# Two-layer attention and MLP in fp32 on one core: half of w_1's loads issued later, the last block's rows kept on chip for layer 2, the first two scores put in other banks

## The chip, the cores and the metric

The kernel runs on one core of one Trainium2 chip, in one launch. Its time is the device time of an execution in microseconds (us); the time before is the median of three runs. Five engines run their own instruction lists in order and meet at semaphores: PE (matrix products, weight loads listed apart as PEld), DVE (vector), ACT (scalar, activation), POOL (GpSimd) and SP, which here only issues DMA transfers.

## The reference

Two layers, each an attention block and an MLP with the same weights, on x of 2048 tokens by 640, all in fp32:

```python
x = x + _A_ref(_layernorm(x), A_wqkv, A_wo)                 # layer 1
x = x + _B_ref(_layernorm(x), B_w1, B_b1, B_w2, B_b2)
x = x + _A_ref(_layernorm(x), A_wqkv, A_wo)                 # layer 2
x = x + _B_ref(_layernorm(x), B_w1, B_b1, B_w2, B_b2)
# _A_ref: qkv = x @ wqkv, 32 heads of 20; o = softmax(q k^T / sqrt(20)) v; o @ wo
# _B_ref: h = x @ w1 + b1 (1536 wide); max(h, 0)^2 @ w2 + b2
```

## The kernel before

**Arithmetic.** Every factor of a product is kept as two parts, high and low, in a reduced fp32 form (`F32R`), and a product is the sum of three products of parts (`THREE`). So nearly all of the work is PE's.

**Stages of one layer.** (1) `qkv`: layer norm of four blocks of 512 tokens (`front`: load four 128-row tiles `x`, statistics at L244 and L245 on DVE and L247 and L248 on POOL, normalise at L252, 20 PE transposes at L398 into banks, and a split into `xnT`), then the projections to q, k and v (`product`, L327; v leaves its bank at L373). The projections of a tile stand in two row halves on PE, and a small ACT copy `mark_t` (L329) hands over between them. (2) Attention: a first pass of scores by queries (L479) only finds the row maxima (L491 on DVE straight from the bank, or L500 on ACT and L508 on DVE for pairs); the second pass computes scores by keys (`score`, L561), exponentials (L568, ACT) and the product with v (`pv`, L573), which accumulates in bank 7. (3) `add_heads`: the out-projection (L289) of four blocks of four row tiles, each row tile in two halves, each half added to the residual row by DVE from its bank (L1154). (4) `mlp`: four blocks of 512 tokens, each in two halves of the 1536: six groups of products with w_1 (L289 again, called by `mlp`), ReLU (L1224, ACT), square (L1225, DVE), split (L256, L257), then products with w_2 (L1239) and adds into the rows (L1250, DVE).

**From the out-projection to the MLP.** The rows of block 0 need layer norm and a turn by 90 degrees before the first w_1 product. `turn_out` does it in ten steps: per row statistics, normalise, a 32x32 transpose by DVE (L1186) into a tile `y`, and four scattered stores `d_t<-y`, issued one step after the transpose. `turn_in` then loads the five `xnT` tiles back (`xnT<-d_t`), in one step, and in five more steps casts each on ACT (L1202) and subtracts (L1203). These steps are a list, and `side()` runs the next one after each bank of the out-projection has been added. In the turn of block 0 this DVE work stands in between DVE's adds, in the order of the program.

**Order and resources.** There is no scheduler: instructions stand on each engine in program order, written out by hand. SP issues all loads and stores named here in its own order, at L76, and a transfer waits there for its data and for one of a small number of lanes. Weights w_1 (15 slots of 512 KB) and w_2 lie in 42 arena slots, with `xnT`, e, q, k and v; rows `x` and `y` share 11 slots of another pool. PSUM has eight banks. `Ring` hands out banks in turn: `ps_st` banks 0 to 3 for the scores by keys, `ps_pj` 4 to 7 for projections, `ps_q` 0 to 3 for maxima and transposes during `qkv`; in attention the maxima rotate over 4, 5, 6 (`sm_ring`). `ps_all` rotates over all eight in stages 3 and 4.

**Names of the change.** `loads` in `layer` lists which weights are loaded before which block of the out-projection; `loads[1]` is the second part of w_1. `ahead` is true in layer 1, where the MLP already prepares layer 2's projections: three of the four blocks are turned through memory during the last MLP block, and the fourth, block 3, is prepared by `second()`, called at the start of layer 2's `qkv`, with `front`, from the rows that the MLP stored to memory (`d_x`).

Of the kernel before, what the change touches and what calls it, by code (L numbers as in the profile page):

```python
# [39 lines left out]
def tile_layers(  # L40
# [29 lines left out]
    def dma(eng, dst, src):  # L70

        if dst.dtype == F32R:
            dst = dst.bitcast(F32)
        if src.dtype == F32R:
            src = src.bitcast(F32)
        eng.dma_start(dst, src)  # L76
# [291 lines left out]
    def end_v(tt, hf, dst):  # L368
        whole = tt in vs
        if not whole:  # L370
            vs[tt] = slot([P, H, 32], F32, "v")
            nc.gpsimd.memset(vs[tt][:, :, DH:], 1.0)
        nc.scalar.copy(  # L373
            vs[tt][:, hf * 16 : hf * 16 + 16, :DH],
            dst[:, :HALF].rearrange("p (h d) -> p h d", d=DH),
        )
        if whole:
            v = vs.pop(tt)
            return lambda: dma(nc.sync, d_v[tt * P : (tt + 1) * P], v)

    def front(tb, x_src, bank, each=1, on_pool=()):

        rows = [row_tile(x_src, tb * 4 + i) for i in range(4)]
        yield 0, False
        mvs = []
        for x in rows:
            mvs.append(stats(x))
            yield 1.1, False
        for n, (x, mv) in enumerate(zip(rows, mvs)):
            normalise(nc.vector, x, mv)  # L390
            yield 0.65, n == 3
        res = []
        for k0 in range(0, KD, each):
            ks = range(k0, min(k0 + each, KD))
            dsts = [bank("xt") for _ in ks]
            for k, dst in zip(ks, dsts):
                for i in range(4):
                    nc.tensor.transpose(  # L398
                        dst[:, i * P : (i + 1) * P], rows[i][:, k * P : (k + 1) * P], ident
                    )  # L400
            for k, dst in zip(ks, dsts):
                t = slot([P, 2, QB], F32R, "xnT")
                (split_on_pool if k in on_pool else split_to)(t[:, 0, :], t[:, 1, :], dst)
                res.append(t)
            if len(res) == KD:
                xt_[tb] = res
                rows.clear()
            yield 0, len(res) < KD
# [132 lines left out]
    def mrows_load(t):  # L541
# [7 lines left out]
            )  # L549
        done.add(t)  # L550

    def score(t, kt, h, es):

        p, par = divmod(h, 2)
        if p not in es:
            es[p] = weights[len(e_n) % len(weights)]
            e_n.append(t)
        dst = ps_st("st")
        b = 64 * par
        assert t in done  # L560
        nc.tensor.matmul(  # L561
            dst,
            k_t[t // NQB, kt // 4][b : b + 62, p, (kt % 4) * P : (kt % 4 + 1) * P],
            q_t[t][b : b + 62, p, :],
            start=True,
            stop=True,
        )
        nc.scalar.activation(es[p][:, par, :], dst, AF.Exp, scale=SCALE)  # L568
# [385 lines left out]
    def attention(first, x_src, first_rows):  # L954
# [135 lines left out]
        def pairs():  # L1090
# [8 lines left out]
            state["debt"] -= n  # L1099
            return n  # L1100

        for o in "abab":
            op(o)
        yield
# [101 lines left out]
    def new_rows():  # L1206
        return [slot([P, 2, QB], F32R, "xnT") for _ in range(KD)]

    def mlp(qb, xnt, x_mid, x_dst, side):

        xs = []
        for fh in range(2):
            hs = []
            for f in range(fh * 6, fh * 6 + 6):
                dst = ps_all("pu")
                chain(dst, [
                    (w_1.piece(f * 10 + hw * KD + k), xnt[k][:, hx, :])
                    for k in range(KD)
                    for hw, hx in THREE
                ])  # L1220
                if qb == NQB - 1:
                    w_1.past(f * 10 + 9)
                r = xtile("r")[:, :QB]
                nc.scalar.activation(r, dst, AF.Relu, bias=b1_t[:, f : f + 1])  # L1224
                nc.vector.tensor_mul(r, r, r)  # L1225
                h = slot([P, 2, QB], F32R, "h")
                split_to(h[:, 0, :], h[:, 1, :], r)
                hs.append(h)
                if fh == 0 and f in (1, 2, 3, 4):
                    x = row_tile(x_mid, qb * 4 + f - 1)  # L1230
                    nc.gpsimd.tensor_add(x, x, b2_t)
                    xs.append(x)
                side()
            f0 = fh * 6

            def part(dst, hf, i, fs):
                for f in fs:
                    for hx, hw in THREE:
                        nc.tensor.matmul(  # L1239
                            dst[:, :HALF],  # L1240
                            hs[f][:, hx, i * P : (i + 1) * P],
                            w_2.piece(at_2(f0 + f, hw, hf)),
                            start=(f == 0 and (hx, hw) == THREE[0]),
                            stop=(f == 5 and (hx, hw) == THREE[-1]),
                        )

            def add(dst, hf, i):
                c = slice(hf * HALF, (hf + 1) * HALF)
                x = xs[i]
                nc.vector.tensor_add(x[:, c], dst[:, :HALF], x[:, c])  # L1250
                r0 = (qb * 4 + i) * P
                if fh == 1 and qb * 4 + i == NKT - 1:
                    dma(nc.sync, x_dst[r0 : r0 + P, c], x[:, c])
                elif fh == 1 and hf == 1:
                    dma(nc.sync, x_dst[r0 : r0 + P, :], x)
                side()

            first_two = [ps_all("y") for _ in range(2)]
            for fs in (range(5), (5,)):
                for i in range(2):  # L1260
                    part(first_two[i], 0, i, fs)
            for i in range(2):
                add(first_two[i], 0, i)
            for hf in range(2):
                for i in range(0 if hf else 2, 4):
                    dst = ps_all("y")
                    part(dst, hf, i, range(6))
                    add(dst, hf, i)
            if fh == 0 and qb == NQB - 1:
                w_2.past(at_2(5, 1, 1))  # L1270

    def layer(first, x_a, x_m, x_e, front_0, ahead):
# [15 lines left out]
        def all_steps():  # L1288
# [3 lines left out]
        xnt, rows = [], []  # L1292
        loads = [
            [(w_1, s) for s in range(8)],
            [(w_1, s) for s in range(8, w_1.n)],
            [(w_2, s) for s in range(5)],
            [(w_2, s) for s in range(5, 10)],
        ]
        for qb in range(NQB):
            if qb + 2 == NQB:  # L1300
                xnt.extend(new_rows())
            add_heads(qb, x_a, x_m, xs, side, rows)
            if qb == 0:
                out_0 = turn_out(d_t[0], rows)
                steps.extend([lambda: next(out_0)] * 10)
                in_0 = turn_in(d_t[0], lambda: xnt)
                steps.extend([lambda: next(in_0)] + [None] * 2 + [lambda: next(in_0)] * 5)
            for sp, s in loads[qb]:
                sp.load(s)
            if qb + 1 == NQB:  # L1310
                all_steps()
# [3 lines left out]
        for qb in range(NQB):  # L1315
            new = []
            plan = [[] for _ in range(28)]

            def put(gen, *sides):
                for i in sides:  # L1320
                    plan[i].append(lambda: next(gen))

            def rows_of(src, tb):
                return lambda i: row_tile(src, tb * 4 + i)

            def to(where):

                def get():
                    where.extend(new_rows())
                    return where  # L1330

                return get

            d = d_t[(qb + 1) % 2]
            if qb + 1 < NQB:
                put(turn_out(d, rows_of(x_m, qb + 1)), *range(4, 14))
                put(turn_in(d, to(new)), 19, *range(22, 27))
            if ahead and qb:
                out_at = range(14, 24) if qb + 1 < NQB else range(2, 12)
                put(turn_out(d_t[1 + qb], rows_of(x_e, qb - 1)), *out_at)  # L1340
            if ahead and qb + 1 == NQB:
                for tb, at in enumerate((4, 14, 19)):
                    xt_[tb] = []
                    sub = nc.gpsimd.tensor_sub if tb == 2 else nc.vector.tensor_sub
                    put(turn_in(d_t[2 + tb], to(xt_[tb]), sub), at, *range(at + 3, at + 8))
                for n in range(5):
                    plan[20 + n].append(lambda n=n: w_qk.load(n))
            steps.extend((lambda p=p: [f() for f in p]) for p in plan)
            mlp(qb, xnt, x_m, x_e, side)
            xnt = new  # L1350
            if qb + 1 < NQB:
                all_steps()
# [4 lines left out]
    def second():  # L1357


        yield from front(3, d_x[1], ps_q, 2, (1, 3))  # L1360

    def constants():

# [97 lines left out]
```

## Time and profile before

| | us |
|---|---|
| median of the runs | 3607.83 |
| the runs | 3604.56, 3607.83, 3613.43 |
| the profiled execution | 3610.41 |
| its span | 3608.6 |
| PE busy in the span | 3583.8 (99%) |
| DVE busy | 2752.8 (76%) |
| ACT busy | 2650.0 (73%) |
| POOL busy | 803.7 (22%) |

A row of the timeline gives the start in us from the span's start, the busy time of the group, the engine, the line and operation, what it writes and reads, its shape and the count of instructions; in brackets stand the idle time of the engine ahead of it, in us, and what ended it. A row of the waits gives the waiting engine, what it wrote, its line, the releaser, and then the whole wait in us, the number of waits and the longest. Of this span 25 us lie outside of PE's busy time; the prediction looks for them by place.

### The profile page before, as it was taken

What the parts mean: (1) busy time and instruction counts of PE and PEld (TensorE: products, weight loads), DVE (VectorE), ACT (ScalarE), POOL (GpSimd) and SP (SyncE); (2) the same over time, 40 slices, a digit from 0 to 9 for tenths busy, and PEclk for the clock granted to TensorE, in tenths of its full rate; (3) what the DMA queues carried; (4) which work ended last, traced back from release to release, by engine and by line L of the source; (5) the groups of instructions that cost most, each with busy time, mean ns of one, the idle gap of its engine ahead of it and who ended that gap; (6) DMA issues with size and microseconds to landing.
All of it is one profiled execution on the core that took longest, in us unless ns stands there. A gap on an engine that the chain in (4) does not pass through costs nothing.

```text
span 3608.6 us, 67689 instructions
## 1 busy us (share of the span) xinstructions
PE 3583.8 (99%) x25562; PEld 2131.5 (59%) x25562; DVE 2752.8 (76%) x5081; ACT 2650.0 (73%) x5152; POOL 803.7 (22%) x880
## 2 busy tenths in 40 slices
PE   9999999999999999999999999999999999999999
PEld 7886434343434345999988963333443434368998
DVE  7877999999999993445567789999999999924443
ACT  3678999999999996122327789999999999942221
POOL 5531434311212211111144201211211211211110
PEclk9999999999999999999999999999999999999999
DMA  8866555323211125834577652222322111367221
GB/s 277 279 225 175 172 139 167 113 67 78 58 47 51 42 90 198 271 86 111 145 253 251 204 153 66 76 72 56 77 72 62 48 41 51 105 214 247 74 77 40
DMA packets 378117, 453.89 MB, mean 126 GB/s; under 512 B 176722, under 2 KB 224082, under 8 KB 377790
## 3 DMA queue, kind: packets, MB, share of 16 engines
q1 hardware_dynamic: 376974, 447.21, 41.4%
q8 instruction: 201, 3.29, 0.4%
q10 hardware_dynamic: 816, 2.36, 0.2%
q14 instruction: 126, 1.03, 0.1%
HBM read 275.14 MB, written 174.30 MB: 125 GB/s over the span
## 4 chain that ended last, share of the span: by engine, by line
PE 93%; DMA 3%; DVE 1%; POOL 1%; SPq 1%; ACT 1%; issue 0%; DVEq 0%; POOLq 0%; ACTq 0%
PE banks L573 27%; PE banks L561 19%; PE banks L479 16%; PE banks L289 12%; PE banks L327 9%; PE banks L1239 9%; SPq L76 1%; DMA q<-d_qk 1%; ACT e L568 0%; DVE bst L244 0%; PE banks L398 0%; DMA d_x<-x 0%; DMA few<-d_s 0%; DMA d_t<-y 0%; DMA o<-d_r 0%
## 5 line engine op out<-in xcount | busy, mean ns | idle before, releaser
L568 ACT ACTIVATE e<-banks 128x512 f32<-128x512 f32 x3968 | 2049.2, 604 | 67.7 <-PE banks L479 6.0
L491 DVE TENSOR_REDUCE mx<-banks 128x1 f32<-128x512 f32 x3076 | 1929.8, 683 | 211.7 <-PE banks L479 141.9
L479 PE MATMUL banks<-k,q 60*128 60x512 f32 x3586 | 1243.7, 428 | 2.9 <-DVE mx L491 1.4
L561 PE MATMUL banks<-q,k 62*128 62x512 f32 x3968 | 1116.6, 433 | 1.0 <-DVE mx L508 0.9
L573 PE MATMUL banks<-e,vg 128*32 128x512 f32 x8192 | 1091.0, 605 | 1.5 <-ACT e L1086 1.5
L561 PEld LDWEIGHTS banks<-q,k 62*128 62x128 f32 x3968 | 583.6, 185 | 656.0 <-ACT e L568 623.9
L479 PEld LDWEIGHTS banks<-k,q 60*128 60x128 f32 x3586 | 581.5, 184 | 292.0 <-DVE mx L491 217.6
L508 DVE CUSTOM_DVE_ANT_0 rl<-banks,rl 128x512 f32<-128x512 f32 x510 | 332.9, 688 | 102.2 <-PE banks L479 93.2
L327 PE MATMUL banks<-xnT,wqk 64*128 64x512 f32 x2400 | 381.1, 395 | 0.6 <-ACT mark_t L329 0.6
L573 PEld LDWEIGHTS banks<-e,vg 128*32 128x32 f32 x8192 | 161.1, 108 | 357.3 <-issue 331.0
L1224 ACT ACTIVATE r<-banks,b_t 128x512 f32<-128x512 f32 x96 | 66.2, 689 | 401.4 <-PE banks L289 378.9
L500 ACT ACTIVATE rl<-banks 128x512 f32<-128x512 f32 x512 | 271.9, 597 | 100.1 <-PE banks L479 93.6
L1239 PE MATMUL banks<-w,h 128*128 128x320 f32 x2304 | 340.4, 309 | 0.0
L1239 PEld LDWEIGHTS banks<-w,h 128*128 128x128 f32 x2304 | 339.1, 188 | 1.2
L289 PE MATMUL banks<-xnT,w 128*128 128x512 f32 x1440 | 329.4, 389 | 0.0
L327 PEld LDWEIGHTS banks<-xnT,wqk 64*128 64x128 f32 x2400 | 286.8, 186 | 35.5 <-issue 2.7
L289 PEld LDWEIGHTS banks<-xnT,w 128*128 128x128 f32 x1440 | 269.7, 188 | 55.2
L271 POOL CAST mr<-nt 128x32 fp32r<-128x32 f32 x64 | 13.4, 209 | 1121.4 <-DVE nt L534 1121.4
L617 POOL TENSOR_TENSOR few<-few,minus_t 128x16 f32<-128x16 f32 x62 | 179.8, 2900 | 232.0 <-DMA few<-d_s 231.9
L327 PE MATMUL banks<-wv,xnT 64*128 64x320 f32 x1920 | 199.9, 307 | 0.9 <-ACT mark_t L329 0.9
L327 PEld LDWEIGHTS banks<-wv,xnT 64*128 64x128 f32 x1920 | 188.2, 185 | 2.7 <-ACT mark_t L329 1.6
L1225 DVE TENSOR_TENSOR r<-r 128x512 f32<-128x512 f32 x96 | 75.6, 787 | 127.1 <-ACT r L1224 122.1
(83 smaller groups left out, 2020.1 us busy)
## 6 DMA issues: line engine op xcount, KB each, us to landing
q<-d_qk SPq DMA_DIRECT2D x242, 240.0 KB
d_qk<-ev SPq DMA_DIRECT2D x80, 512.0 KB
k<-d_qk SPq DMA_DIRECT2D x152, 240.0 KB
x<-d_x SPq DMA_DIRECT2D x88, 320.0 KB
d_qk<-ev SPq DMA_DIRECT2D x80, 256.0 KB
d_o<-ot SPq DMA_DIRECT2D x248, 80.0 KB
ot<-d_o SPq DMA_DIRECT2D x38, 512.0 KB
d_v<-v SPq DMA_DIRECT2D x32, 512.0 KB
```

The costliest lines, as they stand in the source:

```text
L289: nc.tensor.matmul(dst, a, b, start=(n == 0), stop=(n == last))
L327: m = nc.tensor.matmul(ch["dst"][:, :width], *pair, start=first, stop=last)
L479: nc.tensor.matmul(dst, q_t[t][b : b + 60, p, sub * P : (sub + 1) * P], k_t[t // NQB, c][b : b + 60, p, :], start=True, stop=True,)
L491: nc.vector.tensor_reduce(maxima(t)[:, 2 * par + p, sub, c : c + 1], dst, axis=AX.X, op=ALU.max)
L500: nc.scalar.activation(res, dst, AF.Relu)
L508: nc.vector.tensor_tensor_reduce(out=r, in0=dst, in1=r, scale=1.0, scalar=LEAST, op0=ALU.add, op1=ALU.max, accum_out=maxima(t)[:, 2 * par ...
L561: nc.tensor.matmul(dst, k_t[t // NQB, kt // 4][b : b + 62, p, (kt % 4) * P : (kt % 4 + 1) * P], q_t[t][b : b + 62, p, :], start=True, stop ...
L568: nc.scalar.activation(es[p][:, par, :], dst, AF.Exp, scale=SCALE)
L573: nc.tensor.matmul(acc[32 * h : 32 * h + 32, :], v_t[t // NQB, kt // 8][:, kt % 8, 32 * h : 32 * h + 32], es[p][:, par, :], start=(kt == 0 ...
L617: nc.gpsimd.tensor_tensor(few, few, minus_t, op=ALU.pow)
L1225: nc.vector.tensor_mul(r, r, r)
L1239: nc.tensor.matmul(dst[:, :HALF], hs[f][:, hx, i * P : (i + 1) * P], w_2.piece(at_2(f0 + f, hw, hf)), start=(f == 0 and (hx, hw) == THREE[0]),
```

## The change

There are three edits.

1. `loads[1]` is empty. The seven loads of w_1 that stood there (slots 8 to 14) are issued as a step of their own, behind the step that issues the five loads `xnT<-d_t` of block 0, in place of one of the two empty steps there. This holds for both layers.
2. In the last MLP block of layer 1, each row tile, once its last half has been added, gets its statistics, and the row before it is normalised into a new tile `y` (`to_normal`), beside its store to memory. `second()` no longer loads these rows: it normalises the last one and goes on with the transposes (`turns`, split from `front`). Row 15 is stored whole in layer 1, not in two halves.
3. The first two scores of attention go to banks 5 and 6 (`free`), not to `ps_st`, and the copies of the last v tile from its banks are made by DVE, not ACT. This holds for both layers.

```diff
@@ copy of v from its bank
-        nc.scalar.copy(
+        (nc.vector.tensor_copy if tt == NKT - 1 else nc.scalar.copy)(
@@ front
+        yield from turns(tb, rows, bank, each, on_pool)
+
+    def turns(tb, rows, bank, each, on_pool):
...
@@ score
-        dst = ps_st("st")
+        dst = banks[:, free.pop(0), :] if free else ps_st("st")
...
+        free.extend((5, 6))
         for o in "abab":
             op(o)
...
+    rows_3 = []
+
+    def to_normal(x, mv):
+        y = xtile("y")
+        nc.vector.tensor_scalar(y, x, mv[:, 0:1], mv[:, 1:2], op0=ALU.subtract, op1=ALU.mult)
+        return y
...
@@ mlp, add
-                if fh == 1 and qb * 4 + i == NKT - 1:
+                if fh == 1 and last and qb * 4 + i == NKT - 1:
                     dma(nc.sync, x_dst[r0 : r0 + P, c], x[:, c])
                 elif fh == 1 and hf == 1:
                     dma(nc.sync, x_dst[r0 : r0 + P, :], x)
+                    if not last and qb + 1 == NQB:
+                        rows_3.append((x, stats(x)))
+                        if i:
+                            rows_3[i - 1] = to_normal(*rows_3[i - 1])
                 side()
@@ layer
-            [(w_1, s) for s in range(8, w_1.n)],
+            [],
...
-                steps.extend([lambda: next(in_0)] + [None] * 2 + [lambda: next(in_0)] * 5)
+                steps.append(lambda: next(in_0))
+                steps.append(lambda: [w_1.load(s) for s in range(8, w_1.n)])
+                steps.extend([None] + [lambda: next(in_0)] * 5)
...
-            mlp(qb, xnt, x_m, x_e, side)
+            mlp(qb, xnt, x_m, x_e, side, not ahead)
@@ second
-        yield from front(3, d_x[1], ps_q, 2, (1, 3))
+        rows_3[3] = to_normal(*rows_3[3])
+        yield 0, False
+        yield 0, False
+        yield 0, True
+        yield from turns(3, rows_3, ps_q, 2, (1, 3))
```

How this moves instructions stands here at three places; lines behind L389 have other numbers in the changed kernel (L398 is L402, L500 is L504, L568 is L574). A number behind a tile's name tells tiles of one name apart.

On SP, in layer 1's out-projection, the end of the seven w_1 loads and what follows them before the change (`y_15789` is the fourth row of block 0; the loads of `x` are residual rows):

```order
L76 DMA w_15759<-d_w_96 128x1024
L76 DMA w_15761<-d_w_96 128x1024
L76 DMA w_15763<-d_w_96 128x1024
L76 DMA x_15770<-in_A_x_dram 128x640
L76 DMA d_t_106<-y_15789 32x20x32 x4
L76 DMA d_x_111<-x_15562 128x640
L76 DMA x_15812<-in_A_x_dram 128x640
L76 DMA xnT_15765<-d_t_106 128x512
L76 DMA xnT_15766<-d_t_106 128x512
```

and the same place after it:

```order
L76 DMA x_15756<-in_A_x_dram 128x640
L76 DMA d_t_106<-y_15775 32x20x32 x4
L76 DMA d_x_111<-x_15562 128x640
L76 DMA x_15798<-in_A_x_dram 128x640
L76 DMA xnT_15751<-d_t_106 128x512
L76 DMA xnT_15752<-d_t_106 128x512
L76 DMA xnT_15753<-d_t_106 128x512
L76 DMA xnT_15754<-d_t_106 128x512
L76 DMA xnT_15755<-d_t_106 128x512
L76 DMA w_15837<-d_w_96 128x1024
L76 DMA w_15839<-d_w_96 128x1024
```

The five loads `xnT<-d_t` and the fourth row's stores ahead of them now stand before all seven w_1 loads, which follow at once behind them.

On PE, at the start of layer 2's projections, the end of the products that stand ahead of the first transposes of block 3 before the change; the whole piece ahead of them is 72 products L327:

```order
L327 MATMUL banks<-xnT_18326,wqk_18762 128x512
L327 MATMUL banks<-xnT_18326,wqk_18833 128x512
L327 MATMUL banks<-xnT_18326,wqk_18785 128x512
L398 MATMUL banks<-ident,x_18907 128x128
L398 MATMUL banks<-ident,x_18909 128x128
L398 MATMUL banks<-ident,x_18911 128x128
L398 MATMUL banks<-ident,x_18913 128x128
```

and after it, where the piece ahead is 25 products:

```order
L327 MATMUL banks<-xnT_18328,wqk_18762 128x512 x2
L327 MATMUL banks<-xnT_18328,wqk_18785 128x512
L327 MATMUL banks<-xnT_18329,wqk_18757 128x512
L402 MATMUL banks<-ident,y_18868 128x128
L402 MATMUL banks<-ident,y_18899 128x128
L402 MATMUL banks<-ident,y_18930 128x128
L402 MATMUL banks<-ident,y_18940 128x128
```

The 20 transposes come 47 products earlier in PE's order, and read the kept tiles `y` in place of rows loaded from memory.

On ACT, at the start of layer 1's attention, the first exponentials (e, L568) and the copies of the last v tile before the change:

```order
L500 ACTIVATE rl_4740<-banks 128x512
L568 ACTIVATE e_4757<-banks 128x512 x2
L568 ACTIVATE e_4758<-banks 128x512 x2
L373 COPY v_4772<-banks 128x16x20 x2
L568 ACTIVATE e_4759<-banks 128x512
L568 ACTIVATE e_4760<-banks 128x512
```

and after it:

```order
L504 ACTIVATE rl_4740<-banks 128x512
L574 ACTIVATE e_4757<-banks 128x512 x2
L574 ACTIVATE e_4758<-banks 128x512 x2
L574 ACTIVATE e_4759<-banks 128x512
L574 ACTIVATE e_4760<-banks 128x512
```

The two copies have left ACT; on DVE they now stand between the last paired maximum of the projections (L508, now L512) and the first maxima of attention (L491, now L495).

More of the change, by code (lines that the diff above doesn't have):

```diff
@@ L550, in mrows_load @@
         done.add(t)
+    free = []
     def score(t, kt, h, es):
@@ L1207, in new_rows, with mlp @@
         return [slot([P, 2, QB], F32R, "xnT") for _ in range(KD)]
-    def mlp(qb, xnt, x_mid, x_dst, side):
+    rows_3 = []
[3 more added lines that the diff above has]
+        return y
+    def mlp(qb, xnt, x_mid, x_dst, side, last):
         xs = []
```

## The prediction

> **What bounds the kernel now.** I read the page's busy table first: PE is busy for 3583.8 of 3608.6 us, so a change that leaves PE's instructions as they are can gain at most the 24.8 us in which PE is idle, and whatever slow clock follows a gap. All three edits move work of other engines and of SP and remove not one product of PE. So I read PE's waits next; these two groups head them (engine, tile, line, releaser: us, times, longest):
>
> ```profile
> PE banks L398 <- DVE x L252: 5.9, 10, 1.3
> PE banks L289 <- DVE x L1154: 4.6, 2, 2.9
> ```
>
> The second is the out-projection waiting for DVE to empty a bank, once in each layer. The timeline of PE shows where, layer 1 first, layer 2 below:
>
> ```profile
> 1413.54 64.36 PE L289 MATMUL banks<-wo,ot 128*128 128x320 f32 x435
> 1480.76 6.20 PE L289 MATMUL banks<-wo,ot 128*128 128x320 f32 x30 [2.85 <-DVE x L1154]
> 1486.79 13.56 PE L289 MATMUL banks<-xnT,w 128*128 128x512 f32 x59
> ```
>
> ```profile
> 3202.19 64.36 PE L289 MATMUL banks<-wo,ot 128*128 128x320 f32 x435
> 3268.29 4.66 PE L289 MATMUL banks<-wo,ot 128*128 128x320 f32 x30 [1.74 <-DVE x L1154]
> 3272.79 19.45 PE L289 MATMUL banks<-xnT,w 128*128 128x512 f32 x85
> ```
>
> The 30 products before the MLP's first take 6.20 us in layer 1 and 4.66 in layer 2, so the gap isn't all that is lost. The windows of PE after layer 1's gap (us, PE busy, granted clock, DMA share, GB/s) say why:
>
> ```profile
> 1482.00:1484.00 2.00, 2.00 (x10) 0.50 1.03 410
> ```
>
> For some 3.5 us after the gap PE had half its clock, and a product took 0.2 us.
>
> Why DVE was late stands in DVE's and SP's timelines:
>
> ```profile
> 1454.79 3.11 SPq L76 DMA_DIRECT2D d_t<-y  x4
> ...
> 1458.56 4.46 SPq L76 DMA_DIRECT2D w<-d_w  x7
> ...
> 1464.44 8.41 SPq L76 DMA_DIRECT2D d_t<-y  x4
> ...
> 1475.15 2.22 SPq L76 DMA_DIRECT2D xnT<-d_t  x5
> ```
>
> ```profile
> 1479.61 0.69 DVE L1203 TENSOR_TENSOR xnT<-xnT 128x512 fp32r<-128x512 f32 x1 [18.78 <-ACT xnT L1202]
> ```
>
> DVE's first subtraction for `xnT` stands in its queue among the adds that empty the out-projection's banks. It waited 18.78 us for its data, and PE filled the eight banks meanwhile. The data were late because the third row's four stores took SP 3.11 us to issue and the fourth row's, behind seven w_1 loads, 8.41: from the first w_1 load to the first `xnT` load 16.6 us went by.
>
> **Edit 1, w_1 behind the turned rows.** The price is read by cadence, since it holds gap and clock together. A whole stretch of out-projection in the chain of waits gives the undisturbed rate:
>
> ```profile
> 1414.10 61.61 PE banks L289 x420
> ```
>
> That is 0.1467 us a product. The 465 products from 1413.54 should end at 1413.54 + 68.2 = 1481.7; the MLP began at 1486.79, 5.0 late. From 3202.19 they should end at 3270.4; it began at 3272.79, 2.4 late. Sum at stake: 7.4 us.
>
> After the change the fourth row's stores should cost about what the third's did, 3.11, since nothing but a row load stands ahead of them. Stores from about 1460, `xnT` loads at 1464 to 1466, and DVE's subtraction 4.5 us later (1475.15 to 1479.61 now), near 1470. A bank is next needed where PE now stops, 1480.76 - 2.85 = 1477.9. That leaves DVE 8 us for the adds that piled up, about half a microsecond each (a row below). I take the whole 7.4. Its bounds are 0 (the stores are as slow by themselves) and -7.4.
>
> What is late next: SP's seven w_1 loads. They are now behind the `xnT` loads, and w_2's first loads queue behind them. These are the first uses:
>
> ```profile
> 1507.22 21.28 PE L1239 MATMUL banks<-w,h 128*128 128x320 f32 x144
> 1528.33 20.59 PE L289 MATMUL banks<-xnT,w 128*128 128x512 f32 x90
> ```
>
> Slots 8 to 14 of w_1 serve the second half of block 0, 1528.33, and w_2 1507.22; both come 5 us earlier when the gap goes. Twelve loads of 512 KB are 6.3 MB, at the 410 GB/s above 15 us. From 1467 they end near 1483, 17 us before w_2's new need at 1502. So I cost the move at nothing; the cover is the MLP's first 90 products.
>
> The Trainium skill ("TensorE: Matmul & The Clock Gate", "What's actually happening") says the clock is cut after an idle window of about 3.4 us that runs freely and not from the gap on. By that the slow stretch need not follow a gap of 2.85 us in each execution, so the 1.5 us by which layer 1's 30 products exceed layer 2's may be missing in others, and the sum would be 9.9.
>
> **Edit 2, rows kept for layer 2.** Here is PE from the last product of layer 1's MLP on, and DVE's last add of that MLP:
>
> ```profile
> 1819.20 3.71 PE L327 MATMUL banks<-xnT,wqk 64*128 64x512 f32 x30
> 1823.19 5.05 PE L327 MATMUL banks<-xnT,wqk 64*128 64x512 f32 x42 [0.28 <-ACT mark_t L329]
> 1828.59 0.33 PE L398 MATMUL banks<-ident,x 128*128 128x128 f32 x1 [0.34 <-DVE x L252]
> ...
> 1832.23 1.09 PE L398 MATMUL banks<-ident,x 128*128 128x128 f32 x8
> ...
> 1834.51 15.25 PE L327 MATMUL banks<-xnT,wqk 64*128 64x512 f32 x132
> ```
>
> ```profile
> 1819.31 0.49 DVE L1250 TENSOR_TENSOR x<-banks,x 128x320 f32<-128x320 f32 x1 [2.15 <-PE banks L1239]
> ```
>
> From 1819.20 to 1834.51, 15.3 us, PE does 78 products (72, and 6 between transposes) at 15.25/132 = 0.1155, 9.0 us, and 20 transposes at 1.03/8 = 0.128, 2.6. So 3.7 us are lost, mostly waiting for rows that went through memory and back.
>
> After the change the transposes stand behind 25 products, reached at 1819.20 + 2.9 = 1822.1. Three rows are ready by then; the fourth is not. Its chain is add, statistics, normalise, as DVE did it in the turn of block 0:
>
> ```profile
> 1448.46 0.45 DVE L1154 TENSOR_TENSOR x<-banks,x 128x320 f32<-128x320 f32 x1
> ...
> 1450.87 0.61 DVE L252 TENSOR_SCALAR x<-x,mv 128x640 f32<-128x640 f32 x1 [0.57 <-POOL mv L248]
> ```
>
> That is 3.02 us from the add's start, so ready at 1819.31 + 3.02 = 1822.3. But row 3's two POOL steps now run beside the normalise of row 2. These rows show such steps alone (first row) and beside normalises (the others):
>
> ```profile
> 1827.41 0.55 POOL L248 TENSOR_TENSOR mv<-mv,half_t 128x1 f32<-128x1 f32 x1
> 1828.14 0.44 POOL L247 TENSOR_TENSOR mv<-mv,eps_t 128x1 f32<-128x1 f32 x1 [0.18 <-DVE mv L245]
> 1828.66 0.96 POOL L248 TENSOR_TENSOR mv<-mv,half_t 128x1 f32<-128x1 f32 x1
> ```
>
> L248 grew by 0.41, and I add as much again at most half for L247: 0.6 in all, so 1822.9. PE waits 0.8 there, and I leave 0.7 for hand-overs between products and transposes (the 0.28 above is one). So 1.5 of 3.7 stay, a gain of 2.2. The bounds are 0, if the earlier transposes only move the wait, and -3.7. Removed row loads cost SP nothing that PE waits for. The five `xnT` subtractions on POOL now interleave with the statistics; the block that they serve is read 200 products later, 23 us, which hides that.
>
> The Trainium skill ("SBUF — State Buffer", "Who interferes with whom") says DVE and GpSimd share a port pair as an exclusive lock, and that a tensor_scalar can hold it and block the other for the whole instruction. It speaks against this edit: by it each POOL step could wait out a normalise, some 1 us more, and the sum would be 10.4. The trace agrees that the steps stretch, by 0.4 and not by a whole 0.6.
>
> **Edit 3, the start of attention.** Waits of PE for the first banks, ACT around the first exponentials, PE's first product with v, DVE then, and a window in mid attention (us, PE, PEld, DVE, ACT, POOL, clock, DMA, GB/s):
>
> ```profile
> PE banks L561 <- DVE mx L508: 0.9, 2, 0.5
> ```
>
> ```profile
> 320.37 2.06 ACT L568 ACTIVATE e<-banks 128x512 f32<-128x512 f32 x4 [1.28 <-issue]
> 322.29 0.79 ACT L373 COPY v<-banks 128x320 f32<-128x320 f32 x2
> ```
>
> ```profile
> 323.56 0.64 PE L573 MATMUL banks<-e,vg 128*32 128x512 f32 x4
> ```
>
> ```profile
> 321.01 0.69 DVE L491 TENSOR_REDUCE mx<-banks 128x1 f32<-128x512 f32 x1 [1.28 <-PE banks L479]
> ```
>
> ```profile
> 600.00:1000.00 400.00, 399.53 (x2817) 159.22 (x2811) 363.81 (x600) 387.27 (x751) 90.80 (x92) 1.00 0.32 88
> ```
>
> The two waits, one in each layer, go, for banks 5 and 6 are free. On ACT 0.79 us of copies leave the queue between the fourth exponential and the fifth. Later PE is busy for 399.53 of 400 us, so what the start gains stays. At most that is 0.45 + 0.79 = 1.24 a layer. I take 0.9, the copies whole and a fourth of the wait, since later scores still take banks that maxima leave. On DVE a copy like it is nearest the add from a bank (0.49 at 1819.31), two are 1.0, and DVE idles 1.28 there. New waits are at the maxima that reuse banks 5, 6 and 4: for exponentials 1 and 2, and for DVE's copies. Behind the latter stand DVE's next maxima; if DVE's idle time doesn't cover them, this edit gains 0. Both layers: -1.8, bounds 0 and -2.5.
>
> **Sum.** -7.4 - 2.2 - 1.8 = -11.4. The profiled execution took 3610.41 (span 3608.6), so 3599.0 by it. It is 2.6 above the median of the runs, 3607.83; on that basis 3596.4, which I predict.
>
> **Rivals.** (a) The fourth row's scattered stores are slow by themselves, not through the loads ahead. For it: the 8.41 began after the w_1 loads were issued, and 320 KB of small pieces must still land. Against it: the third row's took 3.11. Then half of edit 1 goes, and the time is 3607.8 - 3.7 - 4.0 = 3600.1. (b) The earlier transposes and the copies on DVE turn into new waits, so edits 2 and 3 give nothing: 3607.8 - 7.4 = 3600.4. For it: row 3 is late by my own count. (c) Slower: the w_1 loads, issued late, hold w_2 up past its first use. If they don't start by 1487 (15 us ahead of 1502), PE stops at the MLP's 91st product. As bound I take the seven loads, 3.7 MB at 410 GB/s or 9.0 us, and 1.5 of slow clock, in each layer 10.5: 21 - 11.4 = +9.6, so 3617. Against it: 17 us of slack. (d) The order on SP does not help, as each transfer waits for its lane and the `xnT` loads for the same stores; with 2 and 3 alone, 3603.8.
>
> **How the numbers follow.** Forecast 0.70, (a) 0.11, (b) 0.09, (c) 0.06, (d) 0.04. About 0.3%, 10.8 us here, can be told from no change, so faster means below 3597.0. The forecast lies 0.6 us inside; the terms' bounds take it 2 us further down and the spread of runs either way, so of its 0.70 I count 0.48 as faster, and 0.02 of the rivals (a) and (b). Slower is (c). The range runs from 3589, the sum at its bounds (-13.6) and 5 for the spread of medians, to 3604, which takes in (a), (b) and (d).
>
> **What would show it.** Right: the fourth row's stores at 3 to 4 us on SP; no gap in the out-projection's last 30 products and a clock of 1.00 after; L402 at 1822 to 1824 with waits under 2 us in all; the first L579 a microsecond nearer to the last L327. Wrong: stores again near 8 us; a gap of PE at the first L1253 with a DMA as releaser; waits on `mark_t` or DVE at L402 above 3 us; a gap at the third maximum of attention.

## The result, and the profile after

| | before | after |
|---|---|---|
| median of six runs, us | 3608.52 | 3595.73 |
| lowest to highest | 3604.56 to 3613.43 | 3592.47 to 3597.60 |
| profiled execution, its span | 3610.41, 3608.6 | 3592.47, 3590.7 |

The ratio is 0.9962, with a 95% interval of 0.9951 to 0.9973: by it 13.7 us faster, 9.7 to 17.7; the medians lie 12.8 apart. A second measurement of the changed kernel (run e5 below) gave 0.9969 (0.9958 to 0.9981), 11.2 us. The forecast was 3596.4, a gain of 11.4.

The busy table of the page after shows the same PE instructions in less span:

```profile
span 3590.7 us, 67673 instructions
PE 3574.3 (100%) x25562; PEld 2127.1 (59%) x25562; DVE 2754.5 (77%) x5085; ACT 2648.4 (74%) x5148; POOL 805.8 (22%) x880
```

The waits of PE after. The wait for the out-projection's adds (4.6 us before) is gone, the one at the transposes has 4.0 of 5.9 left, all in layer 1's start; the waits for banks at the first scores have 0.2 of 0.9 left:

```profile
PE banks L402 <- DVE x L252: 4.0, 6, 1.3
PE banks L483 <- DVE mx L495: 2.8, 5, 1.1
...
PE banks L567 <- DVE mx L512: 0.2, 1, 0.2
```

PE's timeline at the out-projection of layer 1, then layer 2; the 465 products now stand in one row without a gap:

```profile
1407.99 68.76 PE L289 MATMUL banks<-wo,ot 128*128 128x320 f32 x465
1476.59 20.59 PE L289 MATMUL banks<-xnT,w 128*128 128x512 f32 x90
...
3186.46 68.76 PE L289 MATMUL banks<-wo,ot 128*128 128x320 f32 x465
3255.06 20.59 PE L289 MATMUL banks<-xnT,w 128*128 128x512 f32 x90
```

SP's timeline in layer 1; the last stores take 3.35 us, and the `xnT` loads begin 2.3 us behind them, as before, but 13 us earlier than before, counted from the first of the 465 products (48.6 us behind it, 61.6 before):

```profile
1450.96 3.35 SPq L76 DMA_DIRECT2D d_t<-y  x4
...
1456.56 2.22 SPq L76 DMA_DIRECT2D xnT<-d_t  x5
1458.82 4.73 SPq L76 DMA_DIRECT2D w<-d_w  x7
```

And PE at layer 2's first transposes, which wait for nothing:

```profile
1809.00 3.25 PE L327 MATMUL banks<-xnT,wqk 64*128 64x512 f32 x25
1812.19 1.09 PE L402 MATMUL banks<-ident,y 128*128 128x128 f32 x8
1813.21 0.49 PE L327 MATMUL banks<-xnT,wqk 64*128 64x512 f32 x2
1813.63 1.09 PE L402 MATMUL banks<-ident,y 128*128 128x128 f32 x8
1814.66 0.73 PE L327 MATMUL banks<-xnT,wqk 64*128 64x512 f32 x3
1815.32 0.66 PE L402 MATMUL banks<-ident,y 128*128 128x128 f32 x4
```

The spans differ by 17.9 us, more than the medians, since 3.3 of it fell where nothing was changed. From the start to the first L479 (L483) took 57.58 before and 54.32 after. PE's granted clock from 24 to 26 us, with the same code and much the same wait ahead (1.34 and 1.31), before and then after:

```profile
24.00:26.00 2.00, 2.00 (x11) 0.60 0.97 380
```

```profile
24.00:26.00 2.00, 2.00 (x16) 1.00 1.01 398
```

That isn't the edits' work: run e5, the changed kernel once more, had a clock of 0.59 in the same window. So one pair of traces can't price the edits, and the runs below were cut to give every stretch many times. The table lists, in us, worked out from PE's timelines: *out 1* and *out 2*, the 465 products of each layer's out-projection to the MLP's first; *turn*, layer 2's first 78 products and 20 transposes (where fewer products stood ahead of the last transpose, the rest are added at 0.115 us each); *proj 1* and *proj 2*, from layer 1's first L479, or the end of *turn*, to the first product with v.

| kernel (edits) | out 1 | out 2 | turn | proj 1 | proj 2 |
|---|---|---|---|---|---|
| before (none) | 73.25 | 70.61 | 15.31 | 265.98 | 282.04 |
| e1 (1) | 68.60 | 68.61 | 16.31 | 266.35 | 281.33 |
| e2 (2) | 70.51 | 70.52 | 12.43 | 266.23 | 283.15 |
| e3 (3) | 70.11 | 70.80 | 16.51 | 264.60 | 281.52 |
| e4 (w_1 split) | 68.61 | 68.61 | 16.49 | 266.05 | 282.29 |
| e6 (1, 2) | 68.61 | 68.61 | 12.43 | 266.15 | 282.14 |
| after (1, 2, 3) | 68.61 | 68.61 | 12.43 | 264.04 | 279.65 |
| e5 (1, 2, 3) | 68.61 | 68.60 | 12.43 | 264.84 | 281.50 |
| e8 (1, 2, 3, w_1 last) | 68.61 | 68.60 | 12.41 | 264.11 | 280.46 |
| e11 (banks of 3) | 71.55 | 70.21 | 16.65 | 265.22 | 281.14 |
| e12 (copies of 3) | 68.88 | 69.72 | 18.17 | 265.58 | 281.12 |
| e9 (w_2 ahead too) | 77.65 | 79.35 | 14.73 | 266.39 | 282.24 |

Each row is one execution, and a stretch that an edit leaves alone still varies from row to row.

### The profile page after: what moved, and what is told of

Read it like the earlier page. It is cut to its first block, busy times and chain, and to the rows that moved or that the text cites. A ratio compares the mean times of both kernels' runs of the same rounds, so it can differ in the third digit from the quotient of the medians.

```text
span 3590.7 us, 67673 instructions
## 1 busy us (share of the span) xinstructions
PE 3574.3 (100%) x25562; PEld 2127.1 (59%) x25562; DVE 2754.5 (77%) x5085; ACT 2648.4 (74%) x5148; POOL 805.8 (22%) x880
## 4 chain that ended last, share of the span: by engine, by line
PE 96%; DVE 2%; DMA 1%; ACT 1%; POOL 0%; issue 0%; SPq 0%; DVEq 0%; ACTq 0%; POOLq 0%
PE banks L579 28%; PE banks L567 20%; PE banks L483 16%; PE banks L289 13%; PE banks L327 10%; PE banks L1253 9%; DVE mx L495 1%; PE banks L1085 0%; DMA q<-d_qk 0%; PE banks L402 0%; DVE bst L244 0%; ACT e L1092 0%; ACT e L574 0%; DMA d_qk<-ev 0%; DVE x L252 0%
## 5 line engine op out<-in xcount | busy, mean ns | idle before, releaser
L574 ACT ACTIVATE e<-banks 128x512 f32<-128x512 f32 x3968 | 2048.9, 603 | 65.6 <-PE banks L483 5.5
L495 DVE TENSOR_REDUCE mx<-banks 128x1 f32<-128x512 f32 x3076 | 1930.7, 684 | 209.0 <-PE banks L483 137.4
L483 PE MATMUL banks<-k,q 60*128 60x512 f32 x3586 | 1243.6, 428 | 2.1 <-DVE mx L495 1.7
L483 PEld LDWEIGHTS banks<-k,q 60*128 60x128 f32 x3586 | 581.5, 184 | 290.6 <-DVE mx L495 217.8
L512 DVE CUSTOM_DVE_ANT_0 rl<-banks,rl 128x512 f32<-128x512 f32 x510 | 332.9, 689 | 102.6 <-PE banks L483 93.2
L327 PE MATMUL banks<-xnT,wqk 64*128 64x512 f32 x2400 | 379.7, 394 | 0.3 <-ACT mark_t L329 0.3
L504 ACT ACTIVATE rl<-banks 128x512 f32<-128x512 f32 x512 | 271.9, 597 | 98.8 <-PE banks L483 93.8
L1253 PE MATMUL banks<-w,h 128*128 128x320 f32 x2304 | 340.4, 309 | 0.0
L1253 PEld LDWEIGHTS banks<-w,h 128*128 128x128 f32 x2304 | 339.2, 188 | 1.2
L327 PEld LDWEIGHTS banks<-xnT,wqk 64*128 64x128 f32 x2400 | 287.0, 185 | 34.0 <-issue 2.2
L327 PE MATMUL banks<-wv,xnT 64*128 64x320 f32 x1920 | 200.2, 307 | 0.9 <-ACT mark_t L329 0.9
L327 PEld LDWEIGHTS banks<-wv,xnT 64*128 64x128 f32 x1920 | 188.0, 185 | 2.7 <-ACT mark_t L329 1.6
```

Source lines behind the costliest of these rows:

```text
L327: m = nc.tensor.matmul(ch["dst"][:, :width], *pair, start=first, stop=last)
L483: nc.tensor.matmul(dst, q_t[t][b : b + 60, p, sub * P : (sub + 1) * P], k_t[t // NQB, c][b : b + 60, p, :], start=True, stop=True,)
L495: nc.vector.tensor_reduce(maxima(t)[:, 2 * par + p, sub, c : c + 1], dst, axis=AX.X, op=ALU.max)
L504: nc.scalar.activation(res, dst, AF.Relu)
L512: nc.vector.tensor_tensor_reduce(out=r, in0=dst, in1=r, scale=1.0, scalar=LEAST, op0=ALU.add, op1=ALU.max, accum_out=maxima(t)[:, 2 * par ...
L1253: nc.tensor.matmul(dst[:, :HALF], hs[f][:, hx, i * P : (i + 1) * P], w_2.piece(at_2(f0 + f, hw, hf)), start=(f == 0 and (hx, hw) == THREE[0]),
```

## The experiments

**Each edit alone: e1, e2, e3.** The edits are the hunks of the diff, one at a time, in the kernel before.

> The kernel before with edit 1 alone (seven w_1 loads behind the five xnT loads, both layers). Theory: edit 1 is most of the gain, because the fourth row's stores no longer stand behind w_1. The 465 products of the out-projection then take 68.6 us in both layers, as in the changed kernel (73.2 and 70.6 before), and the time falls by 6.6 us, ratio 0.9982; by 5 if layer 1's slow clock is not in every execution of before. Rival: the scattered stores are slow by themselves and the gap closed only because edits 2 and 3 moved other things: 70 us or more, gain under 3.

> The kernel before with edit 2 alone (rows of block 3 kept on chip for layer 2). Theory: layer 2's 20 transposes no longer wait, 12.4 us for 78 products and 20 transposes (15.3 before), and the time falls by 3 us, to 4 if the waits for q after it shrink too. Out-projection gaps stay. Rival: the earlier transposes wait for row 3 instead, gain 0 to 1. On the clock: if a gap of 2.9 us in layer 1 always brings half the clock, these 30 products take 6.2 us here again; if not, 4.7.

> The kernel before with edit 3 alone (first two scores in banks 5 and 6, last v copies on DVE, both layers). Theory: the first product with v comes about 1 us earlier in each layer, the time falls by 2 us. Rival: the maxima that reuse the banks wait in turn and the gain is given back within the first groups: 0. Out-projection gaps stay; a third look at the clock after layer 1's gap.

Measured: e1 3604.69, ratio 0.9992 (0.9983 to 1.0001); e2 3604.83, 0.9990 (0.9981 to 0.9998); e3 3605.41, 0.9992 (0.9983 to 1.0000). Each moves the stretches it was meant for: both *out* to 68.6 in e1, *turn* to 12.43 in e2, *proj 1* to 264.60 in e3. So the places were right. But the other stretches don't stand still: *out 1* is 70.51 in e2 and 70.11 in e3, where the old order of the loads is kept, and *turn* is 1.0 us longer in e1 and 1.2 in e3 than before (attention 1 took 2.3 us more in e2's trace, which no other run with edit 2 has). Edit 1's size wasn't the expected one: 2.9 us, for 6.6, or for 5 if layer 1's slow clock isn't in every execution; its interval reaches to 6.1. The gaps that stay in e2 and e3 say why. PE's timeline of e2 in layer 1, then of e3:

```profile
1479.09 4.67 PE L289 MATMUL banks<-wo,ot 128*128 128x320 f32 x30 [1.64 <-DVE x L1158]
```

```profile
1477.76 4.66 PE L289 MATMUL banks<-wo,ot 128*128 128x320 f32 x30 [1.24 <-DVE x L1157]
```

The gap is 1.24 or 1.64 there, not 2.85, and no slow clock follows: 30 products take 4.66, not 6.20. Edit 2, on the other hand, meets more than the trace of before showed. PE's turn in e1, where the old order still stands, and the window of its eight transposes (us, PE busy, granted clock, DMA share, GB/s):

```profile
1823.79 0.82 PE L398 MATMUL banks<-ident,x 128*128 128x128 f32 x5 [1.15 <-DVE x L252]
1824.54 0.80 PE L327 MATMUL banks<-xnT,wqk 64*128 64x512 f32 x2
1825.27 1.97 PE L398 MATMUL banks<-ident,x 128*128 128x128 f32 x8
```

```profile
1824.50:1827.00 2.50, 2.50 (x11) 0.50 0.70 267
```

Eight transposes take 1.97 us at half the clock, 1.09 before. The turn is 16.3 to 18.2 us in e1, e3, e4, e11 and e12, whose clock falls there; it is 15.31 in the execution that I had and 14.73 in e9, whose clock stays at 1.00.

**What made the stores late: e4 and e9.** In e4 the seven loads stay ahead of the stores with a quarter of the bytes; in e9 five more stand with them.

```diff
# e4
-                sp.load(s)
+                sp.load(s, 0, 256 if qb == 1 else None)   # columns 0 to 256
...
+                steps.append(lambda: [w_1.load(s, 256) for s in range(8, w_1.n)])
# e9
-            [(w_1, s) for s in range(8, w_1.n)],
-            [(w_2, s) for s in range(5)],
+            [(w_1, s) for s in range(8, w_1.n)] + [(w_2, s) for s in range(5)],
+            [],
```

> The kernel before, with the seven w_1 loads split: the first 256 of 1024 columns at the old place on SP, the other 768 behind the xnT loads. As many transfers stand ahead of the fourth row's stores as before, with a quarter of the bytes. Theory 'bytes': the stores wait until loads of 3.7 MB have landed; with 0.9 MB they take 3 to 5 us to issue, not 8.4, and the out-projection's 465 products take 68.6 to 69 us, gain 5 to 6.6. Theory 'places': seven transfers ahead on SP cost by their number (4.5 us of issue and the lanes they hold): stores and gap as before, gain under 2.

> The kernel before, with five w_2 loads (2.5 MB) issued directly behind the seven w_1 loads, ahead of the fourth row's stores, in both layers. Theory 'bytes': the turned rows come later by 2.5 MB at some 400 GB/s, 6 us, and all of it is PE idle, so the 465 products of each out-projection take 76 to 77 us (70.1 to 70.8 in kernels with the gap and no slow clock), perhaps 1.5 more for a slow clock; the time rises by 11 to 16 us, ratio 1.003 to 1.0045. Rival: the gap is not set by these bytes: 70 to 71 us, ratio 1.

Measured: e4 3605.59, ratio 0.9988 (0.9978 to 0.9997), with no gap in either layer. SP's timeline of e4:

```profile
1457.90 3.35 SPq L76 DMA_DIRECT2D w<-d_w  x7
1461.30 0.42 SPq L76 DMA_DIRECT2D x<-in_A_x_dram  x1
1461.82 3.58 SPq L76 DMA_DIRECT2D d_t<-y  x4
```

Seven transfers ahead, and yet 3.58 us for the stores: the number of transfers isn't it. From the first of these w_1 loads to the first `xnT` load 9.8 us go by, 16.6 before. e9 took 3626.19, 1.0050 (1.0036 to 1.0064), 16.5 us more by the medians, where I expected 11 to 16. Its PE, layer 1 and layer 2, and the window behind layer 1's gap:

```profile
1484.61 7.16 PE L289 MATMUL banks<-wo,ot 128*128 128x320 f32 x30 [6.28 <-DVE x L1154]
...
3279.81 7.25 PE L289 MATMUL banks<-wo,ot 128*128 128x320 f32 x30 [7.89 <-DVE x L1154]
```

```profile
1486.00:1490.00 4.00, 4.00 (x17) 0.50 1.02 401
```

The out-projections take 77.65 and 79.35, more than the 76 to 77 expected: the gaps grew by some 4 to 6 us, and the slow clock costs another 2.5 in each layer (7.16 for 4.66), which I had put at perhaps 1.5. SP's timeline of layer 1:

```profile
1457.48 9.14 SPq L76 DMA_DIRECT2D w<-d_w  x12
...
1468.86 8.05 SPq L76 DMA_DIRECT2D d_t<-y  x4
...
1479.10 2.22 SPq L76 DMA_DIRECT2D xnT<-d_t  x5
```

From the first w load to the first `xnT` load 21.6 us go by, 5.0 more than before. The stores themselves take no longer (8.05, and 8.41 before): it is the twelve loads ahead of them that take longer, 9.14, and in this stretch SP waits 6.6 us for loads of weights, 2.1 before. e9 adds transfers and bytes at once and so can't tell them apart; e4 does, and shows that the turned rows wait for the bytes ahead. What holds SP up, the lanes or the transfers in flight, stays open.

PE's gap follows the `xnT` loads. Counted from the first of layer 1's 465 products they are issued at 59.5 us in e3 and e12 (gaps of 1.24 and some 0.3), at 61.2 to 61.6 in e2, e11 and before (gaps of 1.64 to 2.85), at 65.1 in e9 (6.28).

**All again, and without edit 3: e5, e6.**

> The changed kernel again, beside the next ones on one chip. If edits 1, 2 and 3 add up (2.9, 3.6 and 2.9 us by their ratios alone), 9 to 10 us faster than before, ratio 0.9974; if the 0.9962 of the first measurement is right, 13 to 14 us, and then the edits are worth more together than alone. The profile shows layer 2's stretch of 78 products and 20 transposes at 12.4 us again, since no wait there leaves room for a slow clock.

> The kernel before with edits 1 and 2, without 3. Theory (each edit removes its own wait): 2 to 3 us slower than the changed kernel, ratio to before 0.998. Both out-projections 68.6 us, transposes 12.4 us, the stretch from the first maxima to the first product with v in layer 1 at 266 us (264.0 in the changed kernel). Rival (edit 3 gives its gain back later): as fast as the changed kernel.

Measured: e5 3596.42, 0.9969 (0.9958 to 0.9981); e6 3599.87, 0.9978 (0.9969 to 0.9987). Edit 3 gives 3.4 us on top of the others, and the three ratios alone sum to 9.4: within the intervals, which reach 3 us and more to either side, the edits add up, and there is no sign that they work on one another.

**Slack of the moved loads: e8.**

```diff
         for s in range(10, w_2.n):
             w_2.load(s)
+        for s in range(8, w_1.n):
+            w_1.load(s)
```

> The changed kernel, but the seven w_1 loads issued after all of w_2's, some 25 us later. It asks how much slack the moved loads had (17 us by the prediction for w_2, more for w_1 whose first use is near 1518). Theory: loads of 3.7 MB issued from about 1490 land by 1502, before their use: same time as the changed kernel, out-projections 68.6, no gap of PE before the second half of the first MLP block. Rival (the prediction's slower case): PE stops there for 5 to 10 us in each layer, 10 to 20 us slower than the changed kernel.

Measured: 3596.36, 0.9968 (0.9956 to 0.9980), as the changed kernel. SP's and PE's timelines:

```profile
1479.64 16.41 SPq L76 DMA_DIRECT2D w<-d_w  x18
...
1498.97 21.28 PE L1253 MATMUL banks<-w,h 128*128 128x320 f32 x144
1520.09 10.16 PE L289 MATMUL banks<-xnT,w 128*128 128x512 f32 x44
```

The last of the 18 loads is issued by 1496.1, 24 us ahead of the second half's first product, and PE doesn't stop. This tests the slack of w_1 alone, since w_2 stands ahead of it here. For w_2 the changed kernel itself is the test: its first product with w_2 (L1253, at 1497.02) follows the 90 products from 1476.59 without a gap.

**The two halves of edit 3: e11, e12.**

> The kernel before with the first half of edit 3 alone: the first two scores in banks 5 and 6. Theory: PE's waits of 0.48 and 0.44 us for banks go, a gain of about 1 in sum at most; the copies still stand between exponentials 4 and 5 on ACT, so the first product with v comes 0.3 us earlier or not at all. Rival: this half carries the 1.5 us of layer 1.

> The kernel before with the other half of edit 3 alone: the last v copies on DVE. Theory: exponentials 5 and on come 0.8 us earlier and the first product with v with them, most of edit 3's 1.5 us in layer 1. Rival: DVE's first maxima start later by the two copies and PE waits for them instead: nothing.

Measured: e11 3606.32, 0.9989 (0.9980 to 0.9998); e12 3607.77, 1.0000 (0.9990 to 1.0009). In *proj 1* the banks bring 1.0 us and the copies 0.6 under the 266.19 of the six kernels with neither; the four with both, 1.8. My expectations gave the banks too little and the copies too much, and e12's whole time shows no gain. In layer 2 the same stretches scatter by 1 us and more, and don't tell the halves apart.

**A version that might be faster still: e7, e10.** What is left of the waits at L402 is in layer 1's start. e7 puts the transposes 16 products later; e10 keeps PE's order and interleaves DVE's steps.

```diff
# e7, in front, of the changed kernel
-            yield 0.65, n == 3
+            yield 0.65, False
+        yield 0, False
+        yield 0, True
# e10, in front, of the changed kernel
+        for n in range(8):
+            if n < 4:
+                mvs.append(stats(rows[n]))
+            if 2 <= n < 6:
+                normalise(nc.vector, rows[n - 2], mvs[n - 2])
+            yield 1.1 if n < 4 else 0.65, n == 7
```

> The changed kernel with the transposes of layer 1's three later blocks two steps (16 products, about 1.9 us) later in PE's order. Theory: PE's six waits of 4.0 us there vanish, and with the gaps the slow clock that cost the profiled execution of before 3.3 us in this place; the first maxima come near 50 us (54.3 changed, 57.6 before) and the time falls by 3.5 to 5 us under the changed kernel, ratio to before 0.995 or lower. Rival: the turned rows come too late for the projections and the wait moves: no gain.

> The changed kernel with DVE's statistics and normalises of layer 1's three later blocks interleaved (statistics of row n, then normalise of row n-2), PE's order unchanged. Theory: the last row is ready about 1.5 us earlier in each block, PE's 4.0 us of waits there fall to about 1, without the 12 maxima that the later transposes pushed into attention; attention 1 stays at 1089.6 us, the first maxima come near 52 us, the time falls by 3 to 5 us under the changed kernel: ratio to before 0.996. Rival: POOL's steps beside the normalises become slower and the last row is no earlier: the same as the changed kernel.

Measured: e7 3601.58, 0.9983 (0.9974 to 0.9992), 5 us slower than the changed kernel; e10 3599.60, 0.9971 (0.9961 to 0.9980), no faster. In e7 the waits at the transposes did go, and the first product with v came at 316.3 us instead of 318.4 (321.3 in e5), but the first q was then late, and attention 1 took 1098.35 us instead of 1089.62:

```profile
46.79 0.47 PE L485 MATMUL banks<-k,q 60*128 60x512 f32 x1 [2.17 <-DMA q<-d_qk]
```

The order of the program tells where: the planner now fits 565 maxima into layer 1's projections, 577 in the changed kernel, and leaves 12 more to attention. At DVE's 0.69 each these 12 are 8.3 us, near the 8.7, but DVE's busy time in attention grew by 6.3 only; the cause wasn't tried apart. In e10 the last row came no earlier, and PE's waits at L402 grew from 4.0 us to 5.1. DVE's and POOL's timelines:

```profile
37.20 1.54 DVE L252 TENSOR_SCALAR x<-x,mv 128x640 f32<-128x640 f32 x1 [0.44 <-POOL mv L248]
```

```profile
34.61 1.29 POOL L274 TENSOR_TENSOR ev<-r,ev 128x512 fp32r<-128x512 f32 x1
35.85 0.44 POOL L247 TENSOR_TENSOR mv<-mv,eps_t 128x1 f32<-128x1 f32 x1
36.37 0.80 POOL L248 TENSOR_TENSOR mv<-mv,half_t 128x1 f32<-128x1 f32 x1
37.14 1.26 POOL L274 TENSOR_TENSOR ev<-kf,ev 128x512 fp32r<-128x512 f32 x1
```

The last row's two POOL steps stand behind one L274 and its normalise runs beside the next, 1.54 us for 0.6. No version here beats the changed kernel.

## Why the prediction was right

The time was right to 0.7 us, and that was in good part luck: all three terms of its sum were mis-sized, edit 1 upwards and edits 2 and 3 downwards, these two past their own bounds of 3.7 and 2.5 (edit 2 by less than its scatter).

- **Edit 1, -7.4: mis-sized, it is -4.0.** The mechanism held step by step: the stores at 3.35 us, `xnT` early, no gap, nothing late behind it (e8). The step that failed is "the price is read by cadence" from one execution. The cadence was itself 0.4 us a layer too fast: 465 products that never stop take 68.61, not 68.2. Over the five kernels that keep the old place the loss is 70.86 - 68.61 = 2.25 in layer 1 (0.3 to 4.6) and 1.76 in layer 2; the one trace had the largest gap and the only slow clock of the five. The Trainium skill ("TensorE: Matmul & The Clock Gate", "What's actually happening") has it that the window runs freely; I drew on it for the 1.5 us of slow clock, put the sum at 9.9 without them, and kept the whole term.
- **Edit 2, -2.2: mis-sized the other way, it is -3.9.** The seven runs without it average 16.31, those with it 12.43. Two parts of that: the residue of 1.5 that I left is 0.9, since the row 3 chain ended at 1812.4, before the transpose that reads it; and the slow clock, absent from my trace, was in the turns of e1, e3, e4, e11 and e12, though not of e9.
- **Edit 3, -1.8: it is -3.2** (1.8 in layer 1, 1.4 in layer 2, the latter with a scatter of 1 and more; the whole time of e3 says 2.9). I took the copies whole and a fourth of the wait for banks, 0.1 a layer; the banks alone bring 1.0 in layer 1. The new waits at the maxima (L491, now L495) are small: 1.7 to 3.4 us in the four runs with edit 3, 1.4 before and in e6.
- **The sum** by these is -11.1. The forecast's -11.4 met it because 3.4 us too many for edit 1 and 1.7 and 1.4 too few for the others nearly cancel. Part of it is the slow clock: in the trace that I read it stood in the out-projection, where no other run with the old order and bytes has it, and not in the turn, where five of the seven have it. Nothing in the prediction made these errors cancel.
- **Rivals.** (a) is out by e4, (d) by e1, (b) by e2 and e6. (c) is out by the changed kernel, where PE has no gap ahead of w_2's first products, and e8 shows that w_1 had more slack still. (The prediction's 17 us of slack are 19 by its own figures, 1502 and 1483.) Beside (c) one thing did come late: DVE now waits for residual rows behind the w_1 loads, but the eight banks hide it (DVE's waits in the changed kernel from 1455 to 1480 us):

```profile
DVE x L1161 <- DMA x<-in_A_x_dram: 7.9, 2, 7.1
```

- **The chance** of 0.50 for over 0.3% faster can't be tested by one result: the gain is just above that line by one measurement (0.38%) and at it by the other (0.31%).

## What to carry to other kernels

A transfer that somebody waits for should not be issued behind megabytes that nobody needs yet; find the first use of each and order the queue by it, then prove the slack by making it worse. A loss that one execution shows beside a gap has a spread of its own: price it from several executions, above all where the granted clock is under 1 after it. Where a planner fits small work around long work, moving one step by two places can cost more elsewhere than the wait was worth.

## What the runs showed of the hardware

The clock fell to half after short waits: in e1 after a wait of 1.15 us, in a stretch of 3.5 us in which PE was busy for 2.05. The same stretch kept its clock in the profiled execution of before and in e9; layer 1's start lost it in the former (0.60) and in e5 (0.59), and not in the profiled execution of the changed kernel. Gaps of 1.24 to 2.66 us in the out-projection left the clock alone in the seven that these runs had between those two, 2.85 once cut it, and 6.28 and 7.89 both did. The Trainium skill ("TensorE: Matmul & The Clock Gate", "What's actually happening") names an idle window of about 3.4 us that runs freely. That the clock varies from execution to execution agrees with the free running; the length of idleness doesn't. What share of activity decides stays open.

In e10 a normalise of 0.6 us that starts 0.06 after a POOL subtraction of 1.26 takes 1.54, some 0.9 more. That fits the shared port of DVE and POOL of which the Trainium skill tells ("SBUF — State Buffer", "Who interferes with whom"), but a wait for the rest of the POOL instruction would have added 1.2; no run here tries it apart.
